# Attention and a gated feed-forward block on one core: two heads' matmuls alternate between array halves, 1 KB input rows, 128-token output tiles across batches, one written order for every engine

## The chip, the core and the metric

The kernel runs on one core of a Trainium2 chip. The core has a matrix engine (TensorE; in the profile PE for its matmuls and PEld for its weight loads), VectorE (DVE), ScalarE (ACT), GpSimd (POOL) and SyncE (SP), which work at the same time and wait for each other by semaphores. The metric is the device time of one execution, in microseconds, lower being better.

## What is computed

The inputs are q, k and v of shape (8 batches, 12 heads, 448 tokens, 64) and three weight matrices. Each head's attention uses a squared ReLU in place of a softmax; then the heads are joined to 768 columns and go through a gated feed-forward block:

```python
scores = scale * np.matmul(q, k.transpose(0, 1, 3, 2))
attn = np.maximum(scores, 0.0) ** 2 / S
x = np.matmul(attn, v)            # to (B*S, H*D) = (3584, 768)
g = x @ w_gate                    # 768 -> 1536
gelu = 0.5 * g * (1.0 + erf(g * inv_sqrt2))
val = x @ w_val                   # 768 -> 1536
out = gelu * val @ w_out          # 1536 -> 768
```

## The kernel before, in words

All inputs are float32 in device memory and are turned to bf16 by the loading DMAs, which GpSimd issues. The weights stay in SBUF: `wg` and `wv` (6 row chunks of 128 by 1536 columns each) and `wo` (12 row chunks of 128 by 768). The work goes in slots, one per batch and one more (`for slot in range(B + 1)`, lines 166 to 181). Slot s computes the attention of batch s and the feed-forward part of batch s-1.

Attention takes two heads (a pair) at a time, six pairs a batch.

- `attn_pair_front` (lines 76 to 115) loads the pair's q, k and v by six DMAs (token c*112+p lies in chunk c, partition p, so a DMA's contiguous run is one token of one head: 64 float32, 256 bytes). Eight full transposes (lines 91 and 93, both heads' 128 columns at once) put q and k with the head dimension on the partitions into one PSUM bank, `tps`, and VectorE copies that to `qkT`; head 0 is then on partitions 0 to 63 and head 1 on 64 to 127. For each head j, four score matmuls (line 103) use the 64 array rows of that head, `tile_position=(64*j, 0)`. Their PSUM tile `sp` is four banks and there is one of it (`bufs=1`). ScalarE applies the ReLU to all four banks in one instruction (line 111, 1792 columns) and VectorE squares it (line 112).
- `attn_pair_back` (lines 117 to 132) does the product with v: four matmuls for head 0 into partitions 0 to 63 of `opsum`, then four for head 1 into 64 to 127 (line 125, array columns `(0, 64*j)`). VectorE scales the sum into `xT` (line 131).
- `ffn12_part` (lines 134 to 150): for each of 12 chunks of 128 feed-forward columns, six matmuls for the gate (`gp`, line 139), six for the value (`vp`, line 144), a Gelu on ScalarE (line 148) and a product on VectorE into `uT` (line 149).
- `ffn3_part` (lines 152 to 164): the 448 tokens of a batch in four tiles of 112, each in two halves of 384 columns, each half 12 matmuls (`rp`, line 158), a copy by ScalarE (line 162) and a store by SyncE (line 164).

`gp`, `vp` and `rp` share a PSUM tag of two banks (`psF`). The order of the instructions on each engine is not the order of the code: the framework's scheduler sets it by its own priorities, so that score matmuls of four and output products of four are put between pieces of the feed-forward groups.

Of the kernel before, what the change touches and what calls it, by code (L numbers as in the profile page):

```python
# [11 lines left out]
def kernel(  # L12
# [10 lines left out]
    nc = tc.nc  # L23
    f32 = mybir.dt.float32
# [5 lines left out]
    SC = 4  # L30
    SCS = S // SC
    NPAIR = H // 2
    d_model, d_ff = moe_w_gate.shape
    KC = d_model // 128
    FC = d_ff // 128
    NTC = 4
    TCS = S // NTC
    OG = 2
    OGS = d_model // OG

    out_scale = 1.0 / (D * S)

    const = ctx.enter_context(tc.tile_pool(name="const", bufs=1))
    ident = const.tile([128, 128], bf16)
    make_identity(nc, ident)

    xt_pool = ctx.enter_context(tc.tile_pool(name="xt", bufs=1))
    xT = [xt_pool.tile([128, B * S], bf16, name=f"xT{i}", tag=f"xT{i}")
          for i in range(KC)]

    w_pool = ctx.enter_context(tc.tile_pool(name="wpool", bufs=1))
    wg = w_pool.tile([128, KC, d_ff], bf16, tag="wg")
    wv = w_pool.tile([128, KC, d_ff], bf16, tag="wv")
    wo = w_pool.tile([128, FC, d_model], bf16, tag="wo")
    wjobs = ([(wg, moe_w_gate, dc) for dc in range(KC)]
             + [(wv, moe_w_val, dc) for dc in range(KC)]
             + [(wo, moe_w_out, fc) for fc in range(FC)])

    def wload_part(i0, i1):
        for wt, wsrc, c in wjobs[i0:i1]:  # L60
            nc.gpsimd.dma_start(wt[:, c, :], wsrc[c * 128:(c + 1) * 128, :])  # L61

    asb = ctx.enter_context(tc.tile_pool(name="attn_sb", bufs=4))
    asb2 = ctx.enter_context(tc.tile_pool(name="attn_sb2", bufs=4))
    fsb = ctx.enter_context(tc.tile_pool(name="ffn_sb", bufs=4))
    fu = ctx.enter_context(tc.tile_pool(name="ffn_u", bufs=2))
    psT = ctx.enter_context(tc.tile_pool(name="psum_T", bufs=1, space=bass.MemoryType.PSUM))
    psS = ctx.enter_context(tc.tile_pool(name="psum_S", bufs=1, space=bass.MemoryType.PSUM))
    psO = ctx.enter_context(tc.tile_pool(name="psum_O", bufs=1, space=bass.MemoryType.PSUM))
    psF = ctx.enter_context(tc.tile_pool(name="psum_F", bufs=2, space=bass.MemoryType.PSUM))  # L70

    uT = [fu.tile([128, FC, S], bf16, name=f"uT{i}", tag="uT") for i in range(2)]

    pending = []

    def attn_pair_front(b, pr):
        h0 = 2 * pr
        q16 = asb.tile([SCS, SC, 2, D], bf16, tag="q16")
        k16 = asb.tile([SCS, SC, 2, D], bf16, tag="k16")
        v16 = asb.tile([SCS, SC, 2, D], bf16, tag="v16")  # L80
        for j in range(2):
            nc.gpsimd.dma_start(  # L82
                q16[:, :, j, :], q[b, h0 + j].rearrange("(c p) d -> p c d", p=SCS))
            nc.gpsimd.dma_start(  # L84
                k16[:, :, j, :], k[b, h0 + j].rearrange("(c p) d -> p c d", p=SCS))
            nc.gpsimd.dma_start(  # L86
                v16[:, :, j, :], v[b, h0 + j].rearrange("(c p) d -> p c d", p=SCS))

        tps = psT.tile([128, 2, SC, 128], bf16, tag="T")
        for c in range(SC):  # L90
            nc.tensor.transpose(tps[:, 0, c, 0:SCS], q16[:, c, :, :],  # L91
                                ident[0:SCS, 0:SCS])
            nc.tensor.transpose(tps[:, 1, c, 0:SCS], k16[:, c, :, :],  # L93
                                ident[0:SCS, 0:SCS])
        qkT = asb.tile([128, 2, S], bf16, tag="qkT")
        nc.vector.tensor_copy(qkT[:, :, :], tps[:, :, :, 0:SCS])  # L96

        attnTs = []
        for j in range(2):
            base = 64 * j  # L100
            sp = psS.tile([SCS, SC, 512], f32, tag="S")
            for c in range(SC):
                nc.tensor.matmul(  # L103
                    sp[:, c, 0:S],
                    qkT[base:base + 64, 1, c * SCS:(c + 1) * SCS],
                    qkT[base:base + 64, 0, :],
                    start=True, stop=True,
                    tile_position=(base, 0))
            rl = asb2.tile([SCS, SC, S], bf16, tag="rl")
            attnT = asb2.tile([SCS, SC, S], bf16, tag="attnT")  # L110
            nc.scalar.activation(rl[:, :, :], sp[:, :, 0:S], AF.Relu)  # L111
            nc.vector.tensor_tensor(attnT[:, :, :], rl[:, :, :],  # L112
                                    rl[:, :, :], op=ALU.mult)
            attnTs.append(attnT)
        pending.append((b, pr, v16, attnTs))

    def attn_pair_back():
        if not pending:
            return
        b, pr, v16, attnTs = pending.pop(0)  # L120
        opsum = psO.tile([128, S], f32, tag="O")
        for j in range(2):
            base = 64 * j
            for c in range(SC):
                nc.tensor.matmul(  # L125
                    opsum[base:base + 64, :],
                    v16[:, c, j, :],
# [84 lines left out]
```

## Time and profile before

| what | value |
|---|---|
| three timed runs | 596.6, 594.84, 595.35 us; median 595.35 |
| span of the profiled execution, first to last instruction | 594.3 us |
| PE busy / share of the span | 567.2 us / 95% |
| ACT, DVE, POOL busy | 239.8, 215.3, 214.1 us |
| mean granted TensorE clock | 0.971 |
| HBM read, written | 47.19 MB, 11.01 MB |

The profiled execution's own total is not given beyond its span; the span lies 0.5 us below the fastest timed run and 1.05 us below the median. In the profile a row of a chain or timeline begins with its start and its length in microseconds, then the engine, the line of the kernel and the tile it writes; `x8` means that eight instructions were merged. "Busy" for PE counts matmuls from start to a modelled end, and matmuls overlap in the pipeline, so the distance from one start to the next (the pitch) tells more of the rate than the length of one.

### The profile page before, as it was taken

Reading aid. Unit: us, or ns where it says so; the run is one execution under the profiler, and the core shown is the slowest. Engines: PE = TensorE matmul, PEld = TensorE weight load, DVE = VectorE, ACT = ScalarE, POOL = GpSimd, SP = SyncE. Lnnn points to the kernel's source line nnn. Section 1 sums busy time; section 2 is a strip of 40 time slices with the busy share of each in tenths; the row PEclk is TensorE's granted clock in tenths of the full one; section 3 lists DMA queues with packets and bytes.
Section 4 is the critical chain, followed back from the end, with each engine's and each line's share of the span. In section 5 each row is a group of like instructions: output and inputs, shape, how many; then the busy total and the mean of one; then the engine's idle time right before and its main releaser. Section 6 shows DMA issues by size and latency. Waiting matters only on the chain.

```text
span 594.3 us, 7611 instructions
## 1 busy us (share of the span) xinstructions
PE 567.2 (95%) x3072; PEld 301.5 (51%) x3072; DVE 215.3 (36%) x288; ACT 239.8 (40%) x258; POOL 214.1 (36%) x318
## 2 busy tenths in 40 slices
PE   3687899999999999999999999999999999999997
PEld 1233344466444754466444754456444754457565
DVE  1232345431544144541455134541445224541220
ACT  2324335442553435442544434452445434543221
POOL 7677663522355035530453125440443223000000
PEclk9996579999999999999999999999999999999999
DMA  9999974744575447563664547464555554002002
GB/s 118 192 183 141 60 47 31 47 54 78 35 47 34 84 47 46 36 59 78 41 44 27 92 49 45 29 44 100 37 38 36 71 71 31 1 1 93 1 1 93
DMA packets 141217, 35.09 MB, mean 59 GB/s; under 512 B 134528, under 2 KB 136064, under 8 KB 141184
## 3 DMA queue, kind: packets, MB, share of 16 engines
q0 software_dynamic: 137088, 23.61, 50.8%
q1 hardware_dynamic: 4096, 11.01, 6.0%
q8 instruction: 24, 0.39, 0.3%
q14 instruction: 9, 0.07, 0.0%
HBM read 47.19 MB, written 11.01 MB: 98 GB/s over the span
## 4 chain that ended last, share of the span: by engine, by line
PE 91%; DMA 5%; POOL 3%; issue 1%; DVE 1%; ACT 0%; POOLq 0%
PE rp L158 21%; PE gp L139 20%; PE vp L144 19%; PE sp L103 14%; PE opsum L125 12%; DMA wv<-in_moe_w_val_dram 3%; PE tps L91 2%; PE tps L93 2%; DMA wg<-in_moe_w_gate_dram 2%; DMA wo<-in_moe_w_out_dram 1%; POOL v L86 0%; POOL k L84 0%; POOL q L82 0%; POOL wo L61 0%; POOL wg L61 0%
## 5 line engine op out<-in xcount | busy, mean ns | idle before, releaser
L111 ACT ACTIVATE rl<-sp 112x1792 bf16<-112x1792 f32 x96 | 159.7, 1664 | 155.3 <-PE sp L103 155.3
L112 DVE TENSOR_TENSOR attnT<-rl 112x1792 bf16<-112x1792 bf16 x96 | 104.6, 1090 | 111.2 <-ACT rl L111 110.4
L139 PE MATMUL gp<-xT,wg 128*128 128x448 bf16 x576 | 133.5, 358 | 2.1 <-DVE xT L131 2.1
L86 POOL DMA_DIRECT2D v<-in_v_dram x96 | 67.4, 705 | 183.1 <-PE opsum L125 106.1
L144 PE MATMUL vp<-xT,wv 128*128 128x448 bf16 x576 | 131.6, 358 | 0.0
L158 PE MATMUL rp<-wo,uT 128*112 128x384 bf16 x768 | 130.5, 327 | 0.0
L158 PEld LDWEIGHTS <-uT 128*112 128x112 bf16 x768 | 97.6, 130 | 30.5 <-issue 7.2
L103 PE MATMUL sp<-qkT 64*112 64x448 bf16 x384 | 100.9, 386 | 9.0 <-ACT rl L111 5.3
L148 ACT ACTIVATE gel<-gp 128x448 bf16<-128x448 f32 x96 | 52.0, 542 | 127.0 <-PE gp L139 125.7
L82 POOL DMA_DIRECT2D q<-in_q_dram x96 | 68.0, 709 | 95.1 <-PE tps L93 48.9
L149 DVE TENSOR_TENSOR uT<-gel,vp 128x448 bf16<-128x448 bf16 x96 | 59.3, 618 | 117.0 <-PE vp L144 117.0
L125 PE MATMUL opsum<-attnT,v 112*64 112x448 bf16 x384 | 88.4, 385 | 1.8 <-DVE attnT L112 1.6
L144 PEld LDWEIGHTS <-wv 128*128 128x128 bf16 x576 | 53.9, 98 | 59.3 <-issue 15.0
L139 PEld LDWEIGHTS <-wg 128*128 128x128 bf16 x576 | 51.9, 98 | 60.6 <-issue 22.5
L103 PEld LDWEIGHTS <-qkT 64*112 64x112 bf16 x384 | 44.3, 135 | 59.1 <-issue 34.6
L131 DVE TENSOR_SCALAR xT<-opsum 128x448 bf16<-128x448 f32 x48 | 30.0, 624 | 105.9 <-PE opsum L125 105.9
L84 POOL DMA_DIRECT2D k<-in_k_dram x96 | 67.9, 707 | 0.7 <-DMA wg<-in_moe_w_gate_dram 0.5
L162 ACT COPY osb<-rp 112x384 f32<-112x384 f32 x64 | 30.6, 478 | 67.8 <-PE rp L158 67.8
L125 PEld LDWEIGHTS <-v 112*64 112x64 bf16 x384 | 33.5, 114 | 43.5 <-issue 29.4
L96 DVE COPY qkT<-tps 128x896 bf16<-128x896 bf16 x48 | 29.6, 616 | 26.0 <-PE tps L93 25.5
L91 PE MATMUL tps<-ident,q 112*128 112x112 bf16 x192 | 29.6, 228 | 9.0 <-DMA q<-in_q_dram 9.0
L91 PEld LDWEIGHTS <-q 112*128 112x128 bf16 x192 | 18.9, 103 | 27.2 <-issue 25.4
(13 smaller groups left out, 64.8 us busy)
## 6 DMA issues: line engine op xcount, KB each, us to landing
out_dram<-osb SPq DMA_DIRECT2D x32, 336.0 KB, 2.7
q<-in_q_dram POOLq DMA_DIRECT2D x96, 56.0 KB, 2.7
k<-in_k_dram POOLq DMA_DIRECT2D x96, 56.0 KB, 2.8
v<-in_v_dram POOLq DMA_DIRECT2D x96, 56.0 KB, 2.8
wg<-in_moe_w_gate_dram POOLq DMA_DIRECT2D x6, 384.0 KB, 6.1
wv<-in_moe_w_val_dram POOLq DMA_DIRECT2D x6, 384.0 KB, 7.0
wo<-in_moe_w_out_dram POOLq DMA_DIRECT2D x12, 192.0 KB, 4.7
```

Of the source, the lines that this page charges most:

```text
L82: nc.gpsimd.dma_start(q16[:, :, j, :], q[b, h0 + j].rearrange("(c p) d -> p c d", p=SCS))
L84: nc.gpsimd.dma_start(k16[:, :, j, :], k[b, h0 + j].rearrange("(c p) d -> p c d", p=SCS))
L86: nc.gpsimd.dma_start(v16[:, :, j, :], v[b, h0 + j].rearrange("(c p) d -> p c d", p=SCS))
L91: nc.tensor.transpose(tps[:, 0, c, 0:SCS], q16[:, c, :, :], ident[0:SCS, 0:SCS])
L103: nc.tensor.matmul(sp[:, c, 0:S], qkT[base:base + 64, 1, c * SCS:(c + 1) * SCS], qkT[base:base + 64, 0, :], start=True, stop=True, tile_po ...
L111: nc.scalar.activation(rl[:, :, :], sp[:, :, 0:S], AF.Relu)
L112: nc.vector.tensor_tensor(attnT[:, :, :], rl[:, :, :], rl[:, :, :], op=ALU.mult)
L125: nc.tensor.matmul(opsum[base:base + 64, :], v16[:, c, j, :], attnTs[j][:, c, :], start=(c == 0), stop=(c == SC - 1), tile_position=(0, base))
L139: nc.tensor.matmul(gp[:, :], wg[:, dc, fc * 128:(fc + 1) * 128], xT[dc][:, tsl], start=(dc == 0), stop=(dc == KC - 1))
L144: nc.tensor.matmul(vp[:, :], wv[:, dc, fc * 128:(fc + 1) * 128], xT[dc][:, tsl], start=(dc == 0), stop=(dc == KC - 1))
L149: nc.vector.tensor_tensor(uT[bb % 2][:, fc, :], gel[:, :], vp[:, :], op=ALU.mult)
L158: nc.tensor.matmul(rp[:, :], uT[bb % 2][:, fc, tc4 * TCS:(tc4 + 1) * TCS], wo[:, fc, g * OGS:(g + 1) * OGS], start=(fc == 0), stop=(fc == ...
```

## The change

The computation and its tile shapes in the feed-forward part's first half stay as they are. The rest is written anew.

- **Inputs.** `load_heads` loads several heads by one DMA, token 4*p+c going to chunk c of partition p, so that a contiguous run is four tokens, 256 float32 or 1 KB in memory. The whole batch stays in one buffer for each of q, k and v, with two buffers. Batch 0 comes pair by pair, batch 1 in three parts between the weights, later batches whole at the start of the feed-forward part two batches ahead. The token order that follows is undone by the stores, which write every fourth row.
- **Weights.** `wg` and `wv` come in six column chunks of 256, each pair of chunks being what two of the feed-forward chunks need; `wo` in four parts.
- **Transposes.** Sixteen of 64 columns in place of eight of 128, alternating between array columns 0 to 63 and 64 to 127.
- **Scores.** Chunk by chunk, head 0 and head 1 in turn, each in its half of the array rows. The PSUM tile `sp` is two banks, one for each head, and there are two of it. ReLU and square work on 896 columns.
- **Values.** Chunk by chunk, head 0 and head 1 in turn, each in its half of the array columns.
- **Output.** `uT` holds two batches, 896 tokens, so that output tiles are 128 tokens: seven of them for two batches in place of eight of 112.
- **Order.** `manual_schedule` keeps the order of the code on each engine. Each pair's attention is two items: the first has the values of the pair before, the transposes of the pair after and half of the scores; the second the other half of the scores. Thirteen items run ahead of any feed-forward work; then twelve items are spread evenly over each batch's feed-forward groups, weighed by 0.189 us and 0.1625 us a matmul.
- **Start.** 48 matmuls on zeros (`warm_up`) stand ahead of the first transpose.

```diff
-        for j in range(2):
-            nc.gpsimd.dma_start(
-                q16[:, :, j, :], q[b, h0 + j].rearrange("(c p) d -> p c d", p=SCS))
...
+    def load_heads(b, h0, h1):
+        for t, src in zip(batch[b], (q, k, v)):
+            nc.gpsimd.dma_start(
+                t[:, h0:h1, :, :],
+                src[b, h0:h1].rearrange("h (p c) d -> p h c d", c=SC))
...
+    def transposes(n):
+        b, pr = divmod(n, NPAIR)
+        q16, k16, _ = batch[b]
+        tps = psT.tile([128, 2, SC, 128], bf16, name="tps", tag="T")
         for c in range(SC):
-            nc.tensor.transpose(tps[:, 0, c, 0:SCS], q16[:, c, :, :],
-                                ident[0:SCS, 0:SCS])
-            nc.tensor.transpose(tps[:, 1, c, 0:SCS], k16[:, c, :, :],
-                                ident[0:SCS, 0:SCS])
+            for i, src in enumerate((q16, k16)):
+                for j in range(2):
+                    rows = slice(64 * j, 64 * j + 64)
+                    nc.tensor.transpose(tps[rows, i, c, 0:P], src[:, 2 * pr + j, c, :],
+                                        ident[0:P, 0:P], tile_position=(0, 64 * j))
...
+    def scores(n, half):
+        t = qkT[n]
+        for c in (2 * half, 2 * half + 1):
+            sp = psS.tile([128, 2, 512], f32, name="sp", tag="S")
+            for j in range(2):
+                rows = slice(64 * j, 64 * j + 64)
+                nc.tensor.matmul(sp[0:P, j, 0:S], t[rows, 1, c * P:(c + 1) * P],
+                                 t[rows, 0, :], start=True, stop=True,
+                                 tile_position=(64 * j, 0))
+            rl = rpool.tile([P, 2, S], bf16, name="rl", tag="rl")
+            nc.scalar.activation(rl[:, :, :], sp[0:P, :, 0:S], AF.Relu)
+            a = apool.tile([P, 2, S], bf16, name="attnT", tag="attnT")
+            nc.vector.tensor_tensor(a[:, :, :], rl[:, :, :], rl[:, :, :], op=ALU.mult)
+            att[n, c] = a
+
+    def values(n):
...
+        for c in range(SC):
+            a = att.pop((n, c))
+            for j in range(2):
+                rows = slice(64 * j, 64 * j + 64)
+                nc.tensor.matmul(op[rows, :], v16[:, 2 * pr + j, c, :], a[:, j, :],
+                                 start=(c == 0), stop=(c == SC - 1),
+                                 tile_position=(0, 64 * j))
+        nc.vector.tensor_scalar_mul(xT[b][:, pr, :], op[:, :], scalar1=out_scale)
+
+    def attn_item(m):
+        n, half = divmod(m, 2)
+        if half == 0:
+            if n > 0:
+                values(n - 1)
+            if n + 1 < NP:
+                transposes(n + 1)
+            if n < NP:
+                scores(n, 0)
+        elif n < NP:
+            scores(n, 1)
...
+    def ffn_items(b):
+        items = [(12 * 0.189, lambda fc=fc: gate_value(b, fc)) for fc in range(FC)]
+        full = (b % 2 + 1) * S // TT
+        done = 0 if b % 2 == 0 else S // TT
+        for t in range(done, full):
+            for g in range(2):
+                items.append((12 * 0.1625, lambda t=t, g=g: out_half(b // 2, t, g)))
+        return items
...
+    for pr in range(NPAIR):
+        load_heads(0, 2 * pr, 2 * pr + 2)
+    load_w12(0)
+    load_w12(1)
+    load_heads(1, 0, 4)
+    load_w12(2)
+    load_w12(3)
+    load_heads(1, 4, 8)
+    load_w12(4)
+    load_w12(5)
+    load_wo(0)
+    load_wo(1)
+    load_heads(1, 8, 12)
+    load_wo(2)
+    load_wo(3)
+
+    warm_up()
+    transposes(0)
+    for m in range(2 * NPAIR + 1):
+        attn_item(m)
...
+        for cst, fn in items:
+            fn()
+            at += cst
+            while due and due[0] <= at:
+                due.pop(0)
+                attn_item(m)
+                m += 1
```

Three places show what that does to the order. On PE, in the steady part, the products with v: `v16` is the pair's v, `attnT` the squared scores, `opsum` or `op` the sum. Before, the end of head 0 and the start of head 1:

```order
L125 LDWEIGHTS v16_1474
L125 MATMUL opsum_1630<-attnT_1498,v16_1474 64x448
L125 LDWEIGHTS v16_1474
L125 MATMUL opsum_1630<-attnT_1507,v16_1474 64x448
L125 LDWEIGHTS v16_1474
L125 MATMUL opsum_1630<-attnT_1507,v16_1474 64x448
```

and of the change, from the second matmul of a chunk to the first of the chunk after the next, where one `attnT` holds one chunk of both heads:

```order
L169 MATMUL op_1222<-attnT_1137,v16_127 64x448
L169 LDWEIGHTS v16_127
L169 MATMUL op_1222<-attnT_1144,v16_127 64x448
L169 LDWEIGHTS v16_127
L169 MATMUL op_1222<-attnT_1144,v16_127 64x448
L169 LDWEIGHTS v16_127
L169 MATMUL op_1222<-attnT_1182,v16_127 64x448
```

Before, an `attnT` is one head's four chunks, and its four matmuls stand together; now each `attnT` is read by two matmuls, one for each head.

Also on PE, from the transposes (`tps`) to the scores (`sp`) of a pair. Before, at the first pair of a batch, where a gate group (`gp`) comes between and the scores stand four to a head:

```order
L91 LDWEIGHTS q16_1674
L91 MATMUL tps_1683<-ident_58,q16_1674 128x112
L93 LDWEIGHTS k16_1675
L93 MATMUL tps_1683<-ident_58,k16_1675 128x112
L139 LDWEIGHTS wg_75
L139 MATMUL gp_1712<-xT0_66,wg_75 128x448
```

and of the change:

```order
L138 MATMUL tps_1113<-ident_97,q16_618 64x112
L138 LDWEIGHTS k16_619
L138 MATMUL tps_1113<-ident_97,k16_619 64x112
L138 LDWEIGHTS k16_619
L138 MATMUL tps_1113<-ident_97,k16_619 64x112
L150 LDWEIGHTS qkT_1025
L150 MATMUL sp_1132<-qkT_1025 112x448
L150 LDWEIGHTS qkT_1025
L150 MATMUL sp_1132<-qkT_1025 112x448
L150 LDWEIGHTS qkT_1025
L150 MATMUL sp_1139<-qkT_1025 112x448
```

Each transpose now writes 64 partitions, each source chunk is taken twice (once for each head), and the scores, which belong to the pair before that of the transposes, come two to a PSUM tile right behind them.

On ACT, in the steady part, ReLU (`rl`), Gelu (`gel`) and output copy (`osb`). Before:

```order
L111 ACTIVATE rl<-sp 112x1792 x2
L148 ACTIVATE gel<-gp 128x448 x2
L111 ACTIVATE rl<-sp 112x1792 x2
L148 ACTIVATE gel<-gp 128x448
L111 ACTIVATE rl<-sp 112x1792
L162 COPY osb<-rp 112x384
L111 ACTIVATE rl<-sp 112x1792
L162 COPY osb<-rp 112x384 x7
```

and of the change:

```order
L154 ACTIVATE rl<-sp 112x896 x2
L203 ACTIVATE gel<-ff 128x448
L221 COPY osb<-ff 128x384
L154 ACTIVATE rl<-sp 112x896 x2
L221 COPY osb<-ff 128x384
L154 ACTIVATE rl<-sp 112x896 x2
L221 COPY osb<-ff 128x384 x2
```

The last copies of a batch stood seven in a row; now ReLUs of half the width, two to an item, stand between Gelus and copies through the whole batch.

More of the change, by code (lines that the diff above doesn't have):

```diff
@@ L53 @@
[L53 to L70, printed above, removed]
@@ L117, in attn_pair_back @@
[L117 to L127, printed above, removed]
-                    attnTs[j][:, c, :],
-                    start=(c == 0), stop=(c == SC - 1),
-                    tile_position=(0, base))
-        nc.vector.tensor_scalar_mul(xT[pr][:, b * S:(b + 1) * S], opsum[:, :],
-                                    scalar1=out_scale)
@@ L166 @@
[L166 to L181 removed]
+    warm = const.tile([128, 512], bf16)
```

216 lines of the change are left out of this document (131 added, 85 removed).

## The prediction

> **What bounds the kernel now.** I read the page first (busy time, slices, the chain that ended last), then cut the span into stages, then took the chain of waits through one steady slot and through the start. The page:
>
> ```profile
> PE 567.2 (95%) x3072; PEld 301.5 (51%) x3072; DVE 215.3 (36%) x288; ACT 239.8 (40%) x258; POOL 214.1 (36%) x318
> PEclk9996579999999999999999999999999999999999
> GB/s 118 192 183 141 60 47 31 47 54 78 35 47 34 84 47 46 36 59 78 41 44 27 92 49 45 29 44 100 37 38 36 71 71 31 1 1 93 1 1 93
> PE 91%; DMA 5%; POOL 3%; issue 1%; DVE 1%; ACT 0%; POOLq 0%
> ```
>
> PE is 91% of the chain; ACT and DVE have more than half their time free. So time is to be read from what PE does, stage by stage: the start, the first slot with feed-forward work, one of six equal slots, and the last slot without attention.
>
> ```profile
> 0.00:47.80 47.80, 28.77 (x94) 11.69 (x95) 11.71 (x14) 12.94 (x9) 35.08 (x60) 1.00 1.27 164
> 47.80:77.60 29.80, 26.06 (x86) 10.40 (x86) 10.91 (x15) 11.80 (x8) 19.51 (x30) 0.50 1.03 84
> 77.60:140.85 63.25, 63.23 (x351) 33.99 (x351) 23.69 (x32) 27.36 (x30) 24.70 (x36) 0.97 0.60 52
> 276.30:344.02 67.72, 67.69 (x385) 36.49 (x386) 26.82 (x36) 29.55 (x32) 25.02 (x36) 1.00 0.55 52
> 547.20:594.30 47.10, 42.95 (x241) 26.42 (x240) 8.08 (x13) 10.36 (x20) 0.00 (x0) 1.00 0.12 37
> ```
>
> The columns are window, length, busy PE, PEld, DVE, ACT, POOL, then granted clock, DMA share, GB/s. 77.6 + 63.25 + 6 x 67.72 + 47.1 = 594.3, the whole span. In a steady slot PE never stops, so a slot is the sum of its matmul pitches. The chain in that slot gives them:
>
> ```profile
> 276.30 1.24 PE gp L139 x6
> 277.54 1.14 PE vp L144 x6
> 278.68 1.14 PE gp L139 x6
> 279.81 1.14 PE vp L144 x6
> 280.95 0.05 PE tps L91
> 288.26 1.42 PE opsum L125 x8
> 291.21 0.89 PE sp L103 x4
> 296.42 0.87 PE opsum L125 x4
> 330.98 12.16 PE rp L158 x74
> 343.14 0.89 PE opsum L125 x8
> ```
>
> From 277.54 to 280.95 three groups of six take 3.41, so a feed-forward matmul of 448 columns takes 3.41/18 = 0.189 us; an output matmul of 384 columns 12.16/74 = 0.164; a transpose of 112 columns 0.05. Groups in half the array have a surcharge: a gate group behind one takes 1.24, not 1.14, and four score matmuls 0.89, not 4 x 0.189 = 0.76. So changing between whole array and halves costs about 0.10 each way. The last line is the one that matters: eight value matmuls in 0.89, against 1.42 for eight and 0.87 for four elsewhere. There the array ran the two heads side by side, as four pairs of 0.19 and one surcharge, although the code has them one head after the other. So side-by-side work in column halves is priced in this trace; it just happens at one pair of heads in six. For scores (row halves) no row shows it.
>
> The slot then divides: 144 feed-forward matmuls of 0.189 = 27.2; 96 output matmuls of 0.164 = 15.8; the remaining 24.7 is attention, 4.1 us a pair of heads.
>
> The start is another matter:
>
> ```profile
> 51.19 1.74 PE sp L103 x4
> 52.93 1.65 PE opsum L125 x4
> 50.10 0.09 PE tps L91
> 9.17 1.74 PE L103 MATMUL sp<-qkT 64*112 64x448 bf16 x4 [0.72 <-DVE qkT L96]
> 18.08 8.37 DMA wv<-in_moe_w_val_dram
> 7.64 0.25 PE L93 MATMUL tps<-ident,k 112*128 112x112 bf16 x1 [0.83 <-DMA k<-in_k_dram]
> ```
>
> Four scores take 1.74 there, twice the steady price, at a granted clock of 0.50 (47.8 to 77.6). The row at 9.17 has the same 1.74 where the window says 1.00: the clock record is missing there and the matmuls themselves say half. So for its first 77.6 us the kernel does six pairs on a half-speed array, waiting for DMAs as at 18.08. Its first load of k was there at 7.6.
>
> **The change part by part.**
>
> *Feed-forward, first half.* Same matmuls: 1152 x 0.189 = 217.7 us.
>
> *Output.* 28 tiles x 2 x 12 = 672 matmuls in place of 768: 672 x 0.164 = 110.2, a gain of 15.7. The two-batch `uT` brings no wait: an even batch does the three tiles that are complete.
>
> *Attention, per pair of heads.* Values: the 0.89 row less the surcharge, 0.79. Scores: 8 matmuls in 4 pairs of 0.19, 0.76, and 0.04 for the offset within the pairs. Surcharges: into columns, to rows, to whole, to rows, to whole: five of 0.095, or 0.48. Transposes: now 16 of half width, no row shows them. The lower end is 8 pairs at 0.05, 0.40; the upper is 16 one after another with each load exposed:
>
> ```profile
> L125 PEld LDWEIGHTS <-v 112*64 112x64 bf16 x384 | 33.5, 114 | 43.5 <-issue 29.4
> L103 PEld LDWEIGHTS <-qkT 64*112 64x112 bf16 x384 | 44.3, 135 | 59.1 <-issue 34.6
> L91 PEld LDWEIGHTS <-q 112*128 112x128 bf16 x192 | 18.9, 103 | 27.2 <-issue 25.4
> ```
>
> 48 columns more cost a load 135 - 114 = 21 ns, so 64 columns occupy about 28 ns of the 114, the rest being latency; 16 x (0.05 + 0.028) = 1.25. Loads of 103 ns already hide behind matmuls of 50, so I take 0.50, near the lower end. Sum: 0.79 + 0.80 + 0.48 + 0.50 = 2.57, with 0.03 for the remainder 2.6, against 4.1. With 42 pairs beside feed-forward work that is 109 us; at the transposes' upper end 109 + 42 x 0.75 = 141.
>
> The 128-column load of the transposes at present is the quickest per column of the three rows. The Trainium skill, page "TensorEngine Tiling (Array Packing)", section "Restrictions and Gotchas", says that column tiling excludes the fast weight load; its page "TensorE: Matmul & The Clock Gate", section "LDWEIGHTS", would put 64 columns at 53 ns, so two a pair one after the other at 0.107 in place of 0.05. By that the transposes would take 0.86 a pair and the kernel about 15 us more; the trace does not say, since no row shows half-width transposes.
>
> *ReLU, square, and the written order.* What could make PE wait is ACT:
>
> ```profile
> L111 ACT ACTIVATE rl<-sp 112x1792 bf16<-112x1792 f32 x96 | 159.7, 1664 | 155.3 <-PE sp L103 155.3
> L112 DVE TENSOR_TENSOR attnT<-rl 112x1792 bf16<-112x1792 bf16 x96 | 104.6, 1090 | 111.2 <-ACT rl L111 110.4
> L148 ACT ACTIVATE gel<-gp 128x448 bf16<-128x448 f32 x96 | 52.0, 542 | 127.0 <-PE gp L139 125.7
> L149 DVE TENSOR_TENSOR uT<-gel,vp 128x448 bf16<-128x448 bf16 x96 | 59.3, 618 | 117.0 <-PE vp L144 117.0
> L131 DVE TENSOR_SCALAR xT<-opsum 128x448 bf16<-128x448 f32 x48 | 30.0, 624 | 105.9 <-PE opsum L125 105.9
> L162 ACT COPY osb<-rp 112x384 f32<-112x384 f32 x64 | 30.6, 478 | 67.8 <-PE rp L158 67.8
> ```
>
> Four times the columns cost ACT 1122 ns more, 0.835 a column, so 896 columns take 0.168 + 0.748 = 0.92. An item has two, 1.83, queued ahead of the next Gelu. Walk it: the item's scores end on PE; 1.83 later both ReLUs are done, then the Gelu, at 2.4. On PE a gate and a value group take 2.27 and the surcharge 0.1. The gate bank is wanted again at 2.37, so only where two feed-forward groups follow without an item between does PE wait about 0.1; three or four times a batch. DVE's square of 896 is about 0.62 (nearest rows 1090 for 1792 and 618 for 448); squares end at 2.6, the product with the value by 3.2, wanted at 3.5. Values read squares made a group earlier. So 0.3 us a batch, 2 in all. A batch has 24 x 0.92 + 12 x 0.54 + 7 x 0.48 = 32 of ACT and 30 of DVE in 56 of PE; neither binds.
>
> *Loads.* Bytes are the same. Rate, over the start, against need:
>
> ```profile
> 8.00:44.00 36.00, 26.16 (x84) 10.26 (x84) 10.73 (x13) 9.98 (x6) 24.28 (x39) 1.00 1.40 190
> v<-in_v_dram POOLq DMA_DIRECT2D x96, 56.0 KB, 2.8
> ```
>
> A batch's heads are 12 x 3 x 57 KB = 2.06 MB, a third of that 0.69, a pair of weight chunks 0.79, a `wo` part 0.59. POOL's order puts batch 1's first third at 4.3 MB, its second at 6.6, its last at 10.0. At 190 GB/s, with 3 us to start and land, that is 26, 38 and 56 us. PE wants the first at its sixth pair (12.3 + 5 x 3.8 = 31, by the start below), the second and third with the second and sixth item beside feed-forward work (40 + 7 = 47; 40 + 18 of matmuls + 6 of items = 64). At 164, the mean of the first 47.8 us, the last third is at 64, just in time; at the 141 of the page's fourth slice it is 7 to 10 late. I take none. Later batches come whole. Their DMAs wait on POOL until PE has read the buffer's former content, but nothing else stands behind them there, and they have 57 us of PE to hide behind. The stores become 49 in place of 32 on SP; only the last, of 112 rows as now, lies on the path.
>
> *Start.* The warm-up is 27 matmul times of 512 columns: 5.8 us at full clock, 12.7 at half (0.189 and 1.65/4 = 0.41 for 448 columns, times 512/448). It begins at about 1 us and the first transposes could start at 7.6; I take its end at 11, between the two clocks, so 3 us are lost to it. Then 24 ReLUs of 0.92 with a gap of 0.03 set the pace, 22.8 us, with the first at 12.3; squares, the last values and the first items behind them end at 37. PE needs 2.6 of each 3.8 us at full clock, and 4.6 to 5 at half clock. Before, PE was busy 26.06 of 29.8 us and the clock stayed at 0.50, so I expect it to fall back for part of the time. Whole start at half clock: +7; never: 0. I take 3, so the first feed-forward matmul is at 40, in place of 77.6. The Trainium skill, page "TensorE: Matmul & The Clock Gate", section "Part 1: The HAM clock gate", has the clock fall only after an idle window of some 3.4 us; by that the start would be 37. The trace disagrees: from 47.8 to 77.6 all of PE's idle time together was 3.7 us, and the clock was half.
>
> *Tail.* The last matmul's end is followed by what stands in the rows now:
>
> ```profile
> 584.96 5.21 PE rp L158 x32
> 590.19 0.48 ACT osb L162
> ```
>
> 584.96 + 5.21 = 590.17, so 4.1 us to the end of the span, unchanged.
>
> **Sum.** 40 + 217.7 + 110.2 + 109 + 2 + 4.1 = 483.0 of span, against 594.3. By stages: the start 37.6 us less; a steady slot 27.2 + 13.8 + 15.6 + 0.3 = 57 in place of 67.72; the last slot as before. The median of the runs shown is 1.05 above the span, so I forecast 484 us.
>
> **The rivals.** *Transposes bound by their weight loads:* 1.25 a pair, 42 x 0.75 = 31 more, 515. For it: the row of 64-column loads is not faster than that of 128. Against: long loads hide behind 50 ns matmuls now. Chance 0.12, with part of the way (500) likelier than the whole.
>
> *The change doesn't do what it says for scores:* row halves run one after the other. Scores cost 1.51, +0.75 a pair, 516. For it: no row shows two row halves at once; at 291.21 four scores cost four. Against: those were all of one head. Chance 0.08.
>
> *Late loads in the first batch:* 141 GB/s or less; +7 to +10, 493. For it: DMA's share was above 1 through the start. Against: each packet is now four times as long. Chance 0.10.
>
> *A ready start and cheap transposes:* clock held, transposes 0.40, no waits; 484 - 3 - 4 - 2 - 3 (warm-up ended earlier) = 472. Chance 0.12.
>
> *Slower than before:* the written order makes PE wait for ACT. If a ReLU of 896 columns cost as much as one of 1792 (1.66), the two of an item would hold the next Gelu by 1.5 us more, and PE with it, since the gate's bank is not free: 192 ReLUs x 0.74 = 142 us, 626. It decides from 1.49 a ReLU on (111 us of gain over 192). For it: order on ACT is now fixed and ReLUs stand ahead of Gelus. Against: 542 for 448 columns puts the fixed part at 0.17. Chance 0.02.
>
> The forecast itself keeps 0.56. The range, 466 to 513, leaves out the serial scores (0.08), the upper end of the load-bound transposes (0.04), the slower case (0.02) and what may lie below 466 (0.03), 0.17 in all; it takes in the other cases and, below, the ready start with 6 us to spare. A difference of 0.3%, 1.8 us, is about what a measurement of this kernel tells from none. Every case but the last is faster by far more: faster 0.97, same 0.005, slower 0.025 (the 0.02 and a little for what I don't see).
>
> **What would show each step.** Values in about 0.8 for eight and scores in about 0.4 for four in the chain; transposes of a pair together 0.4 to 0.6; feed-forward starting at 37 to 44; steady batches of 55 to 58 with PE's idle time below 1 us; ReLU at 0.92. Scores at 0.76 for four, transposes above 0.9, waits of PE for ACT above 1 us an item, or DMA waits between 31 and 65 us would make it wrong.

## The result, and the profile after

The changed kernel takes 486.88 us (median of four runs, 486.45 to 487.95) against 595.3 us for the kernel before on the same chip: a ratio of 0.8175, 95% interval 0.8157 to 0.8193. The span of the profiled execution is 486.2 us against 594.3. The forecast was 484 us with a range of 466 to 513.

From the page of the changed kernel, the lines that answer to those shown of before (busy time, granted clock by slices, the chain by engine). In its rows L198 is the gate and value matmuls, L218 the output, L150 scores, L169 values, L138 transposes:

```profile
PE 472.3 (97%) x3408; PEld 240.0 (49%) x3408; DVE 236.2 (49%) x385; ACT 238.8 (49%) x346; POOL 48.7 (10%) x67
PEclk9655999999999999999999999999999999999999
PE 94%; ACT 3%; DVE 2%; issue 1%; ACTq 0%
```

PE is still the chain. DMAs have left it, and ACT and DVE hold 5% of it, where they held 1%. That part lies in the start, whose chain is shown further down; there, in the second to fourth slice, the clock is at half. By stages (window, length, busy PE, PEld, DVE, ACT, POOL, granted clock, DMA share, GB/s): after the warm-up the first pair, the rest of the start, an odd batch, an even one, the last.

```profile
10.55:16.85 6.30, 3.49 (x48) 1.81 (x50) 3.75 (x6) 3.34 (x4) 6.30 (x10) 1.00 1.35 173
16.85:48.95 32.10, 26.86 (x183) 12.84 (x183) 20.01 (x32) 17.09 (x21) 15.97 (x21) 0.50 1.43 194
103.93:161.86 57.93, 57.93 (x434) 29.95 (x433) 29.41 (x49) 29.99 (x45) 3.21 (x4) 1.00 0.37 63
161.86:215.89 54.03, 54.03 (x410) 27.62 (x409) 29.41 (x49) 28.92 (x43) 2.56 (x4) 1.00 0.38 62
438.51:486.20 47.69, 43.01 (x242) 23.40 (x240) 8.08 (x13) 10.37 (x20) 0.00 (x0) 0.98 0.15 42
```

In the two steady batches PE is busy for the whole window. The chain in one of them, one pair of heads from its values to the next feed-forward groups, and two output groups:

```profile
223.50 0.88 PE op L169 x8
224.38 0.39 PE tps L138 x16
224.77 0.52 PE sp L150 x4
225.28 2.38 PE ff L198 x12
227.66 0.52 PE sp L150 x4
228.18 4.65 PE ff L198 x24
253.26 4.01 PE ff L218 x24
```

Every piece is PE, so again a batch is the sum of its pitches. A pair costs 0.88 + 0.39 + 0.52 + 0.52, and 0.11 each time in the feed-forward group behind it (2.38 in place of 12 x 0.189 = 2.27): 2.53 us, where it was 4.1. Two groups behind each other take 4.65 = 24 x 0.189 + 0.11, so PE does not wait for the Gelu between them.

The 108.1 us of span came off in two places. Up to the end of the first batch's feed-forward part it took 140.85 us and takes 103.93, 36.9 less; the next six batches took 6 x 67.72 = 406.3 and take 438.51 - 103.93 = 334.6, 71.7 less; the last stage is 0.6 longer.

### The profile page after: what moved, and what is told of

It reads as the page before. It is cut to its first block, busy times and chain, and to the rows that moved or that the text cites. A ratio compares the mean times of both kernels' runs of the same rounds, so it can differ in the third digit from the quotient of the medians.

```text
span 486.2 us, 8140 instructions
## 1 busy us (share of the span) xinstructions
PE 472.3 (97%) x3408; PEld 240.0 (49%) x3408; DVE 236.2 (49%) x385; ACT 238.8 (49%) x346; POOL 48.7 (10%) x67
## 4 chain that ended last, share of the span: by engine, by line
PE 94%; ACT 3%; DVE 2%; issue 1%; ACTq 0%
PE ff L198 46%; PE ff L218 23%; PE sp L150 10%; PE op L169 8%; PE tps L138 4%; ACT rl L154 2%; DVE attnT L156 2%; PE ff L76 1%; PE sp L76 0%; DVE qkT L141 0%; ACT osb L221 0%; DVE warm L64 0%; ACTq L154 0%
## 5 line engine op out<-in xcount | busy, mean ns | idle before, releaser
L154 ACT ACTIVATE rl<-sp 112x896 bf16<-112x896 f32 x192 | 165.1, 915 | 121.7 <-PE sp L150 121.7
L156 DVE TENSOR_TENSOR attnT<-rl 112x896 bf16<-112x896 bf16 x192 | 120.1, 625 | 103.1 <-ACT rl L154 103.1
L198 PE MATMUL ff<-xT,wg 128*128 128x448 bf16 x576 | 126.3, 356 | 0.0
L198 PE MATMUL ff<-xT,wv 128*128 128x448 bf16 x576 | 124.6, 352 | 0.0
L218 PE MATMUL ff<-wo,uT 128*128 128x384 bf16 x672 | 114.2, 326 | 0.0
L205 DVE TENSOR_TENSOR uT<-gel,ff 128x448 bf16<-128x448 bf16 x96 | 59.7, 622 | 76.7 <-PE ff L198 74.1
L218 PEld LDWEIGHTS <-uT 128*128 128x128 bf16 x672 | 63.8, 98 | 48.7 <-issue 8.1
L198 PEld LDWEIGHTS <-wg 128*128 128x128 bf16 x576 | 51.6, 98 | 63.0 <-issue 21.2
L198 PEld LDWEIGHTS <-wv 128*128 128x128 bf16 x576 | 56.4, 98 | 52.8 <-issue 0.4
L203 ACT ACTIVATE gel<-ff 128x448 bf16<-128x448 f32 x96 | 52.4, 546 | 57.5 <-PE ff L198 57.5
L150 PE MATMUL sp<-qkT 64*112 64x448 bf16 x384 | 62.1, 396 | 5.4 <-ACT rl L154 5.4
L169 PE MATMUL op<-attnT,v 112*64 112x448 bf16 x384 | 51.9, 382 | 2.0 <-DVE attnT L156 2.0
L169 PEld LDWEIGHTS <-v 112*64 112x64 bf16 x384 | 19.3, 112 | 30.9 <-issue 22.7
L150 PEld LDWEIGHTS <-qkT 64*112 64x112 bf16 x384 | 19.6, 131 | 30.0 <-issue 25.9
L121 POOL DMA_DIRECT2D q<-in_q_dram x15 | 12.0, 799 | 172.8 <-PE tps L138 169.3
L138 PE MATMUL tps<-ident,q 112*64 112x112 bf16 x384 | 27.0, 224 | 0.7 <-DVE qkT L141 0.7
L138 PE MATMUL tps<-ident,k 112*64 112x112 bf16 x384 | 27.0, 223 | 0.0
L138 PEld LDWEIGHTS <-q 112*64 112x64 bf16 x384 | 22.5, 117 | 4.3 <-issue 0.8
L138 PEld LDWEIGHTS <-k 112*64 112x64 bf16 x384 | 21.9, 118 | 3.9
```

The costliest lines, as they stand in the source:

```text
L138: nc.tensor.transpose(tps[rows, i, c, 0:P], src[:, 2 * pr + j, c, :], ident[0:P, 0:P], tile_position=(0, 64 * j))
L150: nc.tensor.matmul(sp[0:P, j, 0:S], t[rows, 1, c * P:(c + 1) * P], t[rows, 0, :], start=True, stop=True, tile_position=(64 * j, 0))
L154: nc.scalar.activation(rl[:, :, :], sp[0:P, :, 0:S], AF.Relu)
L156: nc.vector.tensor_tensor(a[:, :, :], rl[:, :, :], rl[:, :, :], op=ALU.mult)
L169: nc.tensor.matmul(op[rows, :], v16[:, 2 * pr + j, c, :], a[:, j, :], start=(c == 0), stop=(c == SC - 1), tile_position=(0, 64 * j))
L198: nc.tensor.matmul(pt[:, 0:S], w[:, dc, o:o + 128], x[:, dc, :], start=(dc == 0), stop=(dc == KC - 1))
```

## The experiments

Theory: in the steady part only PE's pitches count, so that each part of the change is worth the pitches it saves; the start is another regime, a loop of waits through PE, ACT and DVE at half clock. Rivals: the gain is that of the written order, of the larger input rows, or the array finds its pairs unaided. Each kernel below is the changed kernel with one edit, but for one that is the kernel before with one, and the last, which is the changed kernel with two. Ratios are to the kernel before, on the same chip.

### Scores of one head at a time

```diff
-        for c in (2 * half, 2 * half + 1):
+        rows = slice(64 * half, 64 * half + 64)
+        for g in range(2):
...
-            for j in range(2):
-                rows = slice(64 * j, 64 * j + 64)
+            for i in range(2):
+                c = 2 * g + i
```

> An item's four score matmuls are those of one head, so that both use the same half of the array rows; tiles, ReLUs and squares keep their sizes. Theory (the array halves give the gain, and in the steady part nothing but PE's pitches counts): four scores go from 0.52 to about 0.89 us, 0.37 x 84 items = 31 us, and 2 to 5 us more in the start at half clock: 520 to 523 us. Rival (the array would have found the overlap by itself, or the gain is that of the written order): below 492 us.

525.41 us, ratio 0.8811 (0.8797 to 0.8825), 2.4 us above the expectation. The chain of this kernel at a first half:

```profile
223.94 0.89 PE sp L151 x4
```

Scores go from 0.52 to 0.89. An even batch is 58.53 us, 4.5 more, which is 12 x 0.37; the start loses 5.0 and the first batch, with its first part still at half clock, 5.9. The score pairs are worth their pitches, some 31 us in the steady part.

### Values head by head

```diff
-        for c in range(SC):
-            a = att.pop((n, c))
-            for j in range(2):
+        for j in range(2):
+            for c in range(SC):
+                a = att[n, c]
```

> The eight value matmuls of a pair stand as in the kernel before: four of head 0, then four of head 1. Theory (the alternation must be written): they go from 0.88 to 1.4 to 1.6 us, 0.5 to 0.7 x 42 pairs = 22 to 30 us, and 3 to 7 us in the start: 512 to 524 us. Rival (as in the row of the kernel before with eight in 0.89 us, TensorE runs the second head beside the first by itself once all their inputs lie ready): the steady part keeps 0.88, and only the start loses: 487 to 494 us.

495.2 us, ratio 0.8302 (0.8288 to 0.8316). The chain in the steady part:

```profile
221.86 0.89 PE op L169 x8
```

The rival is right in the steady part: the code's order is that of the kernel before, and the eight matmuls take 0.89 all the same. An even batch is 54.43 us, 0.4 more. The loss is in the start, where feed-forward begins at 55.5 us in place of 48.9, a little more than the rival allowed: there the values wait for squares one by one, and head 1's four matmuls come after the last of them.

### Scores head by head within an item

```diff
-        for c in (2 * half, 2 * half + 1):
-            sp = psS.tile([128, 2, 512], f32, name="sp", tag="S")
-            for j in range(2):
+        sps = [psS.tile([128, 2, 512], f32, name="sp", tag="S") for _ in range(2)]
+        for j in range(2):
...
+            for i in range(2):
+                c = 2 * half + i
```

> The four score matmuls of an item stand as two of head 0, then two of head 1; tiles and the rest as changed. Theory (what counts is that both heads' matmuls stand in one uninterrupted group with their inputs ready; the array finds the overlap): 0.52 us for four stay, 485 to 489 us. Rival (for row halves the alternation must be written; three steps of 0.19 in place of two): plus 0.19 x 84 = 16 us, 501 to 504 us.

495.54 us, ratio 0.8302 (0.8281 to 0.8322), which neither expectation gave. The steady part answers the question:

```profile
223.11 0.52 PE sp L151 x4
```

Row halves too overlap without alternation in the code; an even batch is 54.2 us against 54.03. What I had left out is the start: with both score tiles needed before the first of head 1, PE waits for two ReLUs, and a pair there takes 7.2 us in place of 6.0.

### The kernel before with pairs alone

```diff
-    psS = ctx.enter_context(tc.tile_pool(name="psum_S", bufs=1, space=bass.MemoryType.PSUM))
+    psS = ctx.enter_context(tc.tile_pool(name="psum_S", bufs=2, space=bass.MemoryType.PSUM))
...
-        for j in range(2):
-            base = 64 * j
-            sp = psS.tile([SCS, SC, 512], f32, tag="S")
-            for c in range(SC):
+        for c in range(SC):
+            sp = psS.tile([SCS, 2, 512], f32, tag="S")
+            for j in range(2):
+                base = 64 * j
...
-        for j in range(2):
-            base = 64 * j
-            for c in range(SC):
+        for c in range(SC):
+            for j in range(2):
+                base = 64 * j
```

> The kernel before with one part alone: score tiles of two banks with two of them, ReLU and square on 896 columns, and the two heads in turn for scores and values; loads, output tiles, and the scheduler's order stay. Theory (pairs are worth what their pitches say): a pair of heads costs 0.76 + 0.76 + 0.40 and, by the order that the scheduler gives, about ten changes of mode of 0.095, 2.9 us in place of 4.1, so that 42 pairs give 50 us and the slots 60 to 61 us; with the start as before, 540 to 552 us. Rival (without the written order and the other loads PE waits for ACT or data and the gain is lost): 570 us or more.

548.39 us, ratio 0.9188 (0.9161 to 0.9216). A steady slot and the chain in another:

```profile
312.50:374.75 62.25, 62.16 (x386) 32.27 (x385) 28.61 (x48) 29.75 (x44) 25.06 (x36) 1.00 0.60 56
```

```profile
224.29 0.52 PE sp L104 x4
224.80 0.86 PE gp L140 x4
225.66 0.35 PE sp L104 x2
226.02 0.48 PE gp L140 x2
```

A slot is 5.5 us shorter with the old loads, the old output tiles and the scheduler's order. That is less than the 60 to 61 us that I expected; the time is in the expected range because the first 140.85 us, which I had taken as unchanged, shrink to 125.74. The gain of a slot could be more: the scheduler puts scores by twos between parts of gate groups, and each such place costs a change of mode on either side (0.35 for two scores that need 0.19, and gp x2 at 0.48 in place of 0.38).

So of the 36.9 us that the changed kernel saves up to the end of its first batch, 15.1 come with this part alone, without the new loads. Which of the other parts saves the rest, no run separates.

### Scores in four items

```diff
-    def scores(n, half):
+    def scores(n, part):
...
-        for c in (2 * half, 2 * half + 1):
+        for c in (part,):
...
-    for m in range(2 * NPAIR + 1):
+    for m in range(4 * NPAIR + 1):
...
-        due = [(i + 0.5) / (2 * NPAIR) * total for i in range(2 * NPAIR)]
+        due = [(i + 0.5) / (4 * NPAIR) * total for i in range(4 * NPAIR)]
```

> Scores go chunk by chunk, four items a pair in place of two, so that PE changes between whole array and halves 329 times in place of 230; the same matmuls in the same pairs. Theory (each change costs about 0.095 us): plus 99 x 0.095 = 9.4 us, 494 to 498 us (the start may move by 2). Rival (a change is free where the next group's weights are ready, the surcharge belongs to something else): below 490 us.

503.27 us, ratio 0.843 (0.8412 to 0.8449): more than I expected. In an even batch, 55.50 us, PE has no pause, and the 1.5 us over 54.03 are twelve more changes of mode (41 in place of 29, counted along PE's matmuls in the two traces) at 0.12. An odd batch, 61.20 in place of 57.93, has 3.3 more: seventeen more changes, some 2 us, and what this chain shows:

```profile
238.68 0.35 PE sp L150 x2
...
239.05 0.93 ACT rl L154
...
240.00 0.64 DVE attnT L156
...
240.68 0.38 PE op L169 x2
```

At one place an odd batch puts the last scores of a pair right ahead of that pair's values. The chain goes through a ReLU and a square there for 1.6 us; six of the eight values run meanwhile, and PE stands idle for 0.98 us of the batch. So a change of mode costs about 0.12 us, and a value product needs a feed-forward group between it and its scores.

### Output tiles of 112 tokens

```diff
-    TT = 128
+    TT = 112
...
-            nc.tensor.matmul(rp[:, 0:OGS], u[:, fc, cols],
+            nc.tensor.matmul(rp[0:TT, 0:OGS], u[:, fc, cols],
```

> Output tiles of 112 tokens, four to a batch, as before; all else as changed. Theory: 96 output matmuls more at 0.163 us: plus 15.7 us, 502 to 503 us. Rival 1 (ACT copies or stores in the last batch would hide it): below 497 us. Rival 2 (the slower load of 112 columns, 130 ns against 98, holds the matmuls up): above 506 us, with a pitch above 0.166 us.

503.15 us, ratio 0.8437 (0.8418 to 0.8456). The chain:

```profile
260.90 4.04 PE ff L218 x24
```

24 output matmuls take 4.04 against 4.01 with 128 tokens. The slower loads (130 ns against 98) do not matter; the 96 fewer matmuls do, 15.4 us of span.

### Inputs in runs of 256 bytes

```diff
-                src[b, h0:h1].rearrange("h (p c) d -> p h c d", c=SC))
+                src[b, h0:h1].rearrange("h (c p) d -> p h c d", c=SC))
...
-                    "(p c) d -> c p d", c=SC)
+                    "(c p) d -> c p d", c=SC)
```

> Tokens are put as before (chunk c holds tokens c*112+p), so that the inputs come in runs of 256 bytes, four times as many; weights and all else as changed. Theory (the packets are what loads cost): a batch's inputs take about 23 us in place of 11 to 15, so that batch 1's parts come at about 43, 60 and 80 us against needs of 41, 53 and 71: 6 to 10 us of DMA waits in the first batch, 493 to 498 us; later batches unchanged. Rival (bytes are what loads cost, 190 GB/s either way): 485 to 489 us.

486.48 us, ratio 0.8153 (0.8131 to 0.8174): the same as the changed kernel. The DMA rates by slice, of this kernel and of the changed one:

```profile
GB/s 93 156 182 183 195 182 112 147 115 9 1 33 180 91 1 1 98 127 47 0 2 179 112 12 2 58 148 65 1 0 66 66 0 1 2 67 32 1 32 98
```

```profile
GB/s 109 178 196 198 205 200 12 147 111 12 1 34 167 101 1 1 128 93 49 1 4 178 111 11 2 75 119 76 1 0 66 67 0 1 2 67 32 1 32 98
```

In the first six slices, while the queue is full, the long rows load 5 to 17% faster, not twice as fast. PE waits for no load longer than 0.4 us in either kernel, so that the 1 KB rows are worth nothing in this kernel's time. The rival, that bytes are what loads cost, gave the time; its 190 GB/s either way is a little off.

### The scheduler's order

```diff
-    ctx.enter_context(tc.manual_schedule())
```

> The line that keeps the written order is taken out; the framework's scheduler orders the same instructions. Theory (in the steady part PE is the sum of its pitches, the order is worth little there): batches within 1 us of 54.0 and 57.9, the start anything from 36 to 60: 475 to 500 us. Rival (the written order is where the gain came from): above 520 us, with PE waits or scores and values no longer in pairs.

489.01 us, ratio 0.8192 (0.8168 to 0.8217).

```profile
105.23:163.16 57.93, 57.93 (x434) 29.97 (x433) 29.40 (x49) 29.95 (x45) 3.21 (x4) 1.00 0.37 63
163.16:217.19 54.03, 54.03 (x410) 27.62 (x409) 29.40 (x49) 28.89 (x43) 2.56 (x4) 1.00 0.38 62
```

The batches are the same to 0.01 us, and the scheduler keeps the groups of the items: eight values, sixteen transposes and four scores stand together in its chain as in the written order. Only the start differs, by 1.3 us. So keeping the written order did not give the gain. What grouping the code into items gives by itself, no run shows.

### The start: no warm-up

```diff
-    warm_up()
     transposes(0)
```

> The 48 matmuls on zeros at the start are left out. Theory (they delay the first transposes by 3 us and their clock is lost again at 17 us): first transposes at about 7.6, the first pair about 1 us slower at half clock, 484 to 486 us. Rival (they are worth their time): 488 us or more.

485.26 us, ratio 0.8134 (0.8112 to 0.8157). The first transposes come at 4.3 us, earlier than I said. The clock's record begins at 48.5 us only, but in the chain of the start sixteen transposes take 0.75 us, as in the changed kernel at half clock, in place of 0.39. Feed-forward begins at 46.8, two us earlier than with the warm-up. The warm-up is worth nothing here.

### The start: fillers

```diff
         attn_item(m)
+        fill(6)
```

> Six matmuls on zeros (1.3 us at full clock, 2.6 at half) follow each of the first 13 items; their sums are not read. Theory (the clock falls in the start because PE waits in its loop; the loop itself stays): the clock is held, PE's part of the loop halves, a pair takes about 5 us in place of 6.0, feed-forward starts at 41 to 46: 478 to 484 us. Rival (the clock falls for another reason, or the added matmuls cost what the clock gives): 486 to 500 us, with a granted clock of 0.5 up to the first batch.

484.41 us, ratio 0.8124 (0.8099 to 0.8149), 0.4 us above the expectation. The granted clock is 1.000 over the whole run. The loop stays, though:

```profile
23.23 1.40 PE ff L268 x6
...
25.82 0.92 ACT rl L154
...
26.76 0.64 DVE attnT L156
...
27.44 0.38 PE op L169 x2
```

At full clock a pair takes 5.5 us (the next filler begins at 28.73) in place of 6.0. Of that, ACT waits 0.19 us for scores behind the fillers; the other fillers run while PE waits for a square. So the half clock is not the main loss; the loop is.

### The start: values later

```diff
     for m in range(2 * NPAIR + 1):
-        attn_item(m)
+        n, half = divmod(m, 2)
+        if half == 0:
+            transposes(n + 1)
+            scores(n, 0)
+            if n > 0:
+                values(n - 1)
+        else:
+            scores(n, 1)
```

> Only the first 13 items are reordered: the values of a pair come behind the transposes and first scores of the following items, not ahead of them. Theory (in the start PE waits in a loop: last ReLU, its square, the last values, transposes, scores, first ReLU, 6.0 us a pair): the loop is cut, the pace is that of ACT's 3.7 us or of PE at half clock, 4.6 to 5 us a pair; feed-forward starts at 39 to 43 us in place of 48.9, and the time is 477 to 482 us. Rival (the loads or the half clock set the pace): start unchanged, 485 to 489 us.

473.74 us, ratio 0.7947 (0.7924 to 0.7971): better than the changed kernel by more than I expected. Chain, and stages with the same columns as above:

```profile
20.17 0.40 PE sp L150 x2
20.57 0.88 PE op L169 x8
...
22.63 0.92 ACT rl L154
23.59 0.40 PE sp L150 x2
```

```profile
16.24:19.66 3.42, 3.42 (x30) 1.53 (x31) 2.65 (x6) 2.41 (x4) 3.42 (x5) 0.50 1.33 177
19.66:35.05 15.39, 13.15 (x140) 6.47 (x140) 14.78 (x28) 15.09 (x19) 7.17 (x10) 1.00 1.45 197
35.05:89.73 54.68, 54.20 (x411) 27.61 (x409) 29.27 (x49) 29.03 (x43) 11.01 (x15) 1.00 1.20 183
```

A round, from scores to scores, takes 3.42 us: the four ReLUs of a pair, which start a little before the one ahead has ended, and nothing more, with ACT busy 15.09 of 15.39. The clock is at half for 3.4 us only. Feed-forward begins at 35.05.

### Values later, no warm-up

This is the kernel of the last experiment without its warm-up.

> The start with the values later, and without the 48 matmuls on zeros. Theory (the clock rises when PE has work packed closely and falls when it waits in a loop, the warm-up is not what holds it): PE begins at half clock, has 4.6 to 5 us of work a pair and so no pauses, the clock rises within the first pairs, feed-forward starts at 31 to 36 us: 469 to 474 us. Rival (the warm-up is needed to hold the clock): half clock to the end of the start, feed-forward at 40 us or later, 478 us or more.

474.53 us, ratio 0.7958 (0.7936 to 0.7979), 0.5 us above the expectation and the same as with the warm-up within the intervals. Feed-forward begins at 34.3 us, and the clock rises at 18.7 without any matmul on zeros. These last two are the fastest kernels of the study, 2.8 and 2.7% ahead of the changed one.

## Why the prediction was right, and where it was not

*What bounds the kernel, and the pairs.* Right. The term for a pair was 2.6 us and the pair takes 2.53, a feed-forward matmul has the 0.189 it was given, and an output matmul 0.163 ((4.01 - 0.11)/24) in place of 0.164. Two sizes inside were off in opposite ways: a change of mode costs 0.11 to 0.14 with the offset within a pair, five of them 0.62 in place of 0.48 + 0.07; the transposes take 0.39 in place of 0.50.

*Transposes.* The lower end was right. Their loads, by group, of the changed kernel:

```profile
L138 PEld LDWEIGHTS <-q 112*64 112x64 bf16 x384 | 22.5, 117 | 4.3 <-issue 0.8
L138 PEld LDWEIGHTS <-k 112*64 112x64 bf16 x384 | 21.9, 118 | 3.9
```

117 ns for 64 columns, where 128 took 103 (means over the whole runs): the loads are slower, and sixteen transposes take 0.39 us all the same. Sixteen loads one after the other would take 1.9 us, so they overlap. The Trainium skill, page "TensorEngine Tiling (Array Packing)", section "Restrictions and Gotchas", says that column tiling excludes the fast weight load, and these rows agree with it. The estimate of 0.86 a pair worked out from the Trainium skill, page "TensorE: Matmul & The Clock Gate", section "LDWEIGHTS", did not come; it took the loads of the two halves one after the other.

*That the change does what it says.* It does, but less of it lies in the words "alternate" and "explicit order" than the prediction assumed. In these runs the array works on two heads' matmuls side by side when they stand in one group with their inputs ready, in either order. The kernel before had one head's four scores in one PSUM tile with a single buffer, so the second head could not be there. That the two-bank tiles are what makes room is inferred from this: no run gave the kernel before the new tiles with its old order.

*ReLU and the written order.* Half a ReLU takes 0.915, as worked out, so the slower rival had no ground. The 2 us of PE waits for Gelu did not come.

*Loads.* Right: PE waits for none longer than 0.4 us. The stores are 56 (eight at each of seven sizes) and not the 49 of the prediction; no wait for one stands in the chain.

*The start.* This is the step of the working that failed: "24 ReLUs of 0.92 with a gap of 0.03 set the pace, 22.8 us". Feed-forward began at 48.9, not 40, and beyond the 44 that was given as the slow end. The chain in the start of the changed kernel, one round:

```profile
23.34 0.75 PE tps L138 x16
24.08 0.57 PE sp L150 x2
...
25.49 0.92 ACT rl L154
...
26.43 0.64 DVE attnT L156
...
27.13 0.90 ACT rl L154
...
28.06 0.64 DVE attnT L156
...
28.73 0.58 PE op L169 x2
29.32 0.75 PE tps L138 x16
```

From transposes to transposes it is 5.98 us, and ACT works 3.35 of it. With no feed-forward group between, values stand right behind their own scores, so PE waits for the last ReLU and its square, and ACT then waits for PE to do values, transposes and scores. I had walked through that queue for the steady part, where a group lies between, and taken the busiest engine's pace for the start. With the values two steps later the pace is 3.42 and the time falls by 13 us, which shows it.

That the total agrees to 3 us is luck, since two errors met: the start came out 8.9 us over, the seven batches with attention 6.3 us under (389.6 against 395.9). Of the 6.3, the waits for Gelu that did not come are 2, and 42 pairs at 2.53 in place of 2.6 are 2.9.

*The clock in the start.* I expected it to fall and allowed 3 us; the fall itself is worth little (the fillers gain 2.5 us, the added matmuls included).

## What to carry to other kernels

Two half-array matmuls overlapped here when both stood ready in one uninterrupted group; give them buffers for that and keep the group whole, since each change between whole array and halves cost about 0.12 us. In a stage where no other work fills PE's queue, follow the dependence once round (matmul, activation, square, matmul) and set its length against the busiest engine's work; if it is longer, put the consumer a step or two later in the queue. Larger DMA rows and a warm-up of the clock were worth nothing here, where neither was what the kernel waited for.

## What the runs showed of the hardware that I had not expected

The order of the code did not decide whether halves overlap: eight values took 0.88 us in turn and 0.89 head by head, four scores 0.52 both ways. Strictly in order, four matmuls in one half and then four in the other would take seven steps of 0.189 (the fourth and the fifth run side by side) and a change of mode, 1.42 us. The kernel before shows both cases. Its chain has 1.42 for the values at 288.26, and its timeline on DVE has, for the square of head 1:

```profile
287.62 1.09 DVE L112 TENSOR_TENSOR attnT<-rl 112x1792 bf16<-112x1792 bf16 x1 [1.04 <-ACT rl L111]
...
332.71 1.09 DVE L112 TENSOR_TENSOR attnT<-rl 112x1792 bf16<-112x1792 bf16 x1 [1.72 <-ACT rl L111]
```

The first square ended at 288.71, with head 0's matmuls under way since 288.2; at 343.14, where eight took 0.89, the last square had ended at 333.80, over 9 us before. The starts of single matmuls agree: head 1's first one starts at 288.77, 0.06 us after its square, and the eight at 343.07 start in four pairs, 13 ns apart within a pair. In the kernel with the values head by head, the eight at 221.79 start in the same way, one with a wait for a square (head 0's, the code's first four) and one without in each pair. So matmuls of one half do pass those of the other in PE's queue. That they do so only past what does not still wait fits both cases, but is argued and not tried by itself. The Trainium skill, page "TensorE: Matmul & The Clock Gate", section "Part 3: Packing small matmuls — row/col tiling", has matmuls in strict order and only weight loads pulled ahead; these rows do not agree with it.

What sets the clock is not the busy share alone. It fell at 16.85 us after a stretch in which PE was busy 3.49 of 6.30 us, in pauses of which none was longer than 0.82 us. Once low, it stayed low with PE busy 26.86 of 32.10, at half clock, where the same work takes longer (sixteen transposes 0.75 us in place of 0.39). In the kernel with the values later it rose after 3.42 us without a pause and then held with 13.15 busy of 15.39. So nearly the same busy share stood beside either state. A stretch without pause does not settle it either. The first row here is from the start of the kernel with the scheduler's order, where the clock stayed at half; the other two follow each other in the start of the kernel with the values head by head, where the clock went from full to half and back to full:

```profile
24.62:55.33 30.71, 30.71 (x153) 10.59 (x149) 16.42 (x29) 19.09 (x21) 13.38 (x17) 0.50 1.40 199
```

```profile
27.35:30.76 3.41, 1.75 (x7) 0.60 (x7) 2.46 (x4) 2.80 (x4) 2.02 (x4) 1.00 1.45 196
30.76:34.18 3.42, 3.32 (x25) 1.93 (x25) 1.29 (x3) 0.28 (x1) 1.17 (x2) 0.50 1.45 197
```

In that last trace the clock changes at 17.11, 27.35, 30.76, 34.18, 37.59 and 58.07 us, all whole multiples of 3.41 us apart. The matmuls in the stretches differ more than the busy time: 153 in 30.71 us left the clock low, 25 in 3.42 were followed by a rise. Whether that is what counts stays open.

The Trainium skill, page "TensorE: Matmul & The Clock Gate", section "Part 1: The HAM clock gate", has the clock fall after an idle window of some 3.4 us and rise after a busy one. The multiples of 3.41 us and the rise after one stretch without pause agree with it; the fall without a long idle window and the 30.71 us at half clock do not. The row that I set against it in the prediction, from 47.8 to 77.6, was the wrong one: the clock was at half there already, so that row shows a clock that did not rise and says nothing of a fall.
